# Attention and channel mixing on one core: every engine's order set by a list scheduler inside the kernel, tiles in fixed rings, v loaded once, the gate in place

## The chip, the cores and the metric

The kernel runs on one core of a Trainium2 chip. A core has five engines with instruction queues of their own: TensorE (PE; its weight loads are shown as PEld), VectorE (DVE), ScalarE (ACT), GpSimd (POOL) and SyncE (SP), which here only issues transfers. Each engine works through its queue in order and waits at semaphores for the others. ACT's queue issues transfers too. The metric is the device time of one execution in microseconds, as the median of several runs.

## The reference

Attention over 8 batches of 12 heads with 448 positions of 64 channels, with an RMS norm on q and k; its output, 8 x 448 x 768, goes through a channel-mixing block with a token shift, a squared ReLU and a sigmoid gate.

```python
def _attn_ref(q, k, v, g_q, g_k) -> np.ndarray:
...
    q_n, k_n = (rmsnorm(q, g_q), rmsnorm(k, g_k))
    scale = 1.0 / np.sqrt(q.shape[-1])
    scores = scale * np.matmul(q_n, k_n.transpose(0, 1, 3, 2))
    scores = scores - np.max(scores, axis=-1, keepdims=True)
    attn = np.exp(scores)
    attn = attn / (np.sum(attn, axis=-1, keepdims=True) + 1e-09)
    return np.matmul(attn, v).astype(np.float32)
...
    x_prev = np.concatenate([np.zeros((B, 1, D), dtype=np.float32), x[:, :-1, :]], axis=1)
    xk = mu_k * x + (1.0 - mu_k) * x_prev
    xr = mu_r * x + (1.0 - mu_r) * x_prev
    k = np.maximum(xk @ w_k, 0.0)
    v = k * k @ w_v
    r = 1.0 / (1.0 + np.exp(-(xr @ w_r)))
    return (r * v).astype(np.float32)
```

d_model is 768 and d_ff 1024. mu_r and w_r are drawn with factors 8 and 6.457. The three weight matrices arrive as 64-bit floats; everything else as 32-bit floats.

## The kernel before, in words

To keep precision, every operand of a large matmul is split into a high and a low half of 16 bits, and each product is made of three matmuls: high by high, high by low, low by high. The work falls into three streams.

**Weights.** `weight_tile` (L394) takes one of 20 column tiles in two halves (40 halves): a load of the raw 64-bit words on ACT's queue, three integer operations on DVE that make 32-bit floats of them (L408 to L410, the conversions), a few matmuls and small operations for a scale, and the split into the two halves (L426 to L432).

**Attention.** Two heads are a pair (48 pairs, six to a batch), four heads a quad (24). `prep` (L162) norms q and k of a quad on ACT, POOL and DVE, splits them (`nat`) and turns them with transposing transfers into `stk`. A pair's scores are 7 tiles of 128 x 448, made in four groups of 2, 2, 2 and 1 tiles, with six matmuls each (`group_scores`, L240); the two heads use the two halves of PE's rows. For each tile DVE takes the maximum (L260), ACT the exponent with its sum (L261), DVE the reciprocal (L273, L274), ACT the high half of the scaled probabilities (L279) and DVE the low half (L280), and SP turns both with a transposing transfer into `pT` (L282, L286). `vprep` (L196) scales and splits v; v is held twice, on partitions 0 to 63 and, shifted by one block, on 64 to 127, loaded by three transfers (L157 to L159). `attend` (L299) multiplies `pT` by v in 22 matmuls, 11 for each head side by side, and ACT writes x (L305).

**MoE**, as the code names it. `mix` (L361) makes the shifted mixtures of x, on POOL, DVE and ACT, six for xk and six for xr in a batch (one for each pair), split again. For each of the eight batches, `moe` (L450) makes eight products of xk with w_k (18 matmuls of 448 columns each, L460), which ACT and POOL turn into the two halves of their square through a scratch tile `kf` (L482 to L485), and then, for every block of 128 tokens and half of the columns, a gate product (18 matmuls of 384 columns), three tanh on ACT (L516), a value product (24 matmuls), one DVE operation that joins them (L519) and one on POOL that scales (L520). Two stores on SP write a block. A batch's MoE is 144 matmuls of 448 columns and 294 of 384 on average, 438 in all, 3504 for the eight batches. The first batch has 396 of them and the second 480, since a block that lies across two batches is done with the second.

**The order.** Three generators are stepped by the class `Stream` (L551) on a clock of steps: attention by `ATT_STEPS`, the weights by `W_RATE` and `W_RATE2`, the MoE of a batch `LAG` after its attention. Inside this, the tile framework's own scheduler orders the instructions of each engine; scores get a priority (`QK_PRIORITY`), and `after` (L236) chains the matmuls of one group. `early_mix` makes two of a batch's six xk mixtures after each of its last groups, and the first MoE product may begin with the first two. PSUM has eight banks: four for scores (`sc`), two for the MoE and the weights (`mm`), one for the attention product and small ones (`av`), and one for statistics (`misc`). Scratch tiles are taken from pools that are opened in turn: `pro` until `NA` weight tiles are done, then `mid`, then, after the last weight, `late`. So `kf` has one buffer in batch 0 and two from batch 1 on.

## Time and profile before

| | |
|---|---|
| median of 3 runs | 1216.83 us (1211.75 to 1223.11) |
| the profiled execution | 1216.88 us, of which 1215.1 us from the first to the last instruction (the span) |
| mean granted TensorE clock | 0.934 |
| moved by transfers | 172.77 MB, 142 GB/s on average |
| of these in packets under 512 bytes | 411200 of 456356 packets |

The page of the profile gives totals, forty slices of the span with each engine's busy share in tenths, transfer queues, and groups of instructions with their mean duration and the idle time before them. "Busy" counts an instruction from start to end, so that instructions which overlap on one engine count once. A matmul is shown for longer than the time in which the next can follow it, so PE's pace is read from start to start. For stretches of the span the profile gives busy time by engine, the granted clock (1.00 is full) and the share of the 16 transfer engines.

### The profile page before, as it was taken

Reading aid. Unit: us, or ns where it says so; the run is one execution under the profiler, and the core shown is the slowest. Engines: PE = TensorE matmul, PEld = TensorE weight load, DVE = VectorE, ACT = ScalarE, POOL = GpSimd, SP = SyncE. Lnnn points to the kernel's source line nnn. Section 1 sums busy time; section 2 is a strip of 40 time slices with the busy share of each in tenths; the row PEclk is TensorE's granted clock in tenths of the full one; section 3 lists DMA queues with packets and bytes.
Section 4 is the critical chain, followed back from the end, with each engine's and each line's share of the span. In section 5 each row is a group of like instructions: output and inputs, shape, how many; then the busy total and the mean of one; then the engine's idle time right before and its main releaser. Section 6 shows DMA issues by size and latency. Waiting matters only on the chain. (4 is left out here: it accounts for less than half of the span.)

```text
span 1215.1 us, 18885 instructions
## 1 busy us (share of the span) xinstructions
PE 996.6 (82%) x5935; PEld 476.4 (39%) x5935; DVE 828.9 (68%) x2357; ACT 794.8 (65%) x1756; POOL 672.3 (55%) x678
## 2 busy tenths in 40 slices
PE   1135545686788899999999999999899799999998
PEld 0012222243344344443444444444444354445464
DVE  4577788887977577676877676857775578666200
ACT  3366668677767767677778776777687477865411
POOL 2644357645558645585657564765586257523821
PEclk9996566888989999999999999999999899999999
DMA  7898889978789878878988897797897887885001
GB/s 160 147 182 169 162 165 218 191 152 151 143 139 161 152 123 162 150 129 158 162 154 154 155 170 141 134 167 146 143 157 129 128 148 135 137 158 90 13 14 39
DMA packets 456356, 172.77 MB, mean 142 GB/s; under 512 B 411200, under 2 KB 452672, under 8 KB 456256
## 3 DMA queue, kind: packets, MB, share of 16 engines
q1 hardware_dynamic: 423328, 132.24, 64.2%
q10 hardware_dynamic: 32928, 39.34, 13.8%
q8 instruction: 46, 0.75, 0.3%
q14 instruction: 54, 0.44, 0.1%
HBM read 61.41 MB, written 11.01 MB: 60 GB/s over the span
## 5 line engine op out<-in xcount | busy, mean ns | idle before, releaser
L261 ACT ACTIVATE sc<-sc,sums 128x448 f32<-128x448 f32 x336 | 201.6, 608 | 108.0 <-DVE sums L260 99.4
L280 DVE SCALAR_TENSOR_TENSOR ph<-sc,sums,ph 128x448 f16<-128x448 f32 x336 | 218.3, 677 | 68.4 <-ACT ph L279 66.1
L238 PE MATMUL sc<-stk 64*128 64x448 f16 (+1 forms) x1152 | 190.3, 380 | 68.3 <-DVE ph L280 45.9
L460 PE MATMUL mm<-wvh,kk 128*128 128x384 f16 x896 | 236.5, 332 | 4.0 <-DVE th L519 4.0
L460 PE MATMUL mm<-xk,wkh 128*128 128x448 f16 x768 | 217.8, 363 | 11.6 <-ACT kf L482 10.1
L260 DVE TENSOR_REDUCE sums<-sc 128x1 f32<-128x448 f32 x336 | 196.3, 613 | 37.3 <-PE sc L238 36.7
L279 ACT ACTIVATE ph<-sc,sums 128x448 f16<-128x448 f32 x336 | 195.2, 642 | 31.9 <-DMA pT<-ph 10.1
L238 PE MATMUL av<-pT,vh 128*64 128x448 f16 x672 | 145.8, 387 | 63.4 <-DMA pT<-ph 49.9
L460 PE MATMUL mm<-wrh,xr 128*128 128x384 f16 x672 | 177.1, 327 | 3.1 <-ACT xr L377 2.4
L460 PEld LDWEIGHTS <-kk 128*128 128x128 f16 x1344 | 126.5, 99 | 111.2 <-issue 36.6
L460 PE MATMUL mm<-wvl,kk 128*128 128x384 f16 x448 | 148.9, 332 | 0.0
L460 PE MATMUL mm<-xk,wkl 128*128 128x448 f16 x384 | 139.2, 363 | 0.0
L189 POOL TENSOR_TENSOR nat<-qk,nat 128x896 f16<-128x896 f32 x48 | 91.3, 1903 | 67.6 <-ACT nat L187 67.6
L238 PEld LDWEIGHTS <-stk 64*128 64x128 f16 (+1 forms) x1152 | 56.0, 100 | 184.1 <-issue 138.9
L170 POOL TENSOR_TENSOR xs<-xs 128x448 f32<-128x448 f32 x48 | 55.7, 1160 | 127.1 <-ACT xs L169 126.8
L460 PEld LDWEIGHTS <-xr 128*128 128x128 f16 x1008 | 93.6, 98 | 78.8 <-issue 16.2
L375 DVE SCALAR_TENSOR_TENSOR df<-x,bsc,df 128x448 f32<-128x448 f32 x90 | 90.3, 1014 | 32.7 <-POOL df L374 32.1
L273 DVE TENSOR_SCALAR sums<-sc 128x1 f32<-128x1 f32 x336 | 49.6, 151 | 89.9 <-ACT sc L261 88.5
L182 POOL TENSOR_TENSOR qk<-qk,ss 128x896 f32<-128x896 f32 x48 | 80.1, 1689 | 54.8 <-DVE ss L70 44.7
L460 PE MATMUL mm<-wrl,xr 128*128 128x384 f16 x336 | 109.7, 327 | 0.0
L460 PEld LDWEIGHTS <-wkh 128*128 128x128 f16 x768 | 73.9, 100 | 91.3 <-issue 35.5
L238 PEld LDWEIGHTS <-vh 128*64 128x64 f16 x672 | 59.5, 117 | 113.7 <-issue 67.3
(117 smaller groups left out, 1576.8 us busy)
## 6 DMA issues: line engine op xcount, KB each, us to landing
vf<-in_v_dram SPq DMA_DIRECT2D x48, 224.0 KB, 3.8
qk<-in_k_dram ACTq DMA_DIRECT2D x48, 224.0 KB, 4.8
qk<-in_q_dram ACTq DMA_DIRECT2D x48, 224.0 KB, 5.1
out_dram<-o SPq DMA_DIRECT2D x56, 192.0 KB, 2.9
vf<-in_v_dram SPq DMA_DIRECT2D x48, 192.0 KB, 3.8
raw<-in_moe_w_k_dram ACTq DMA_DIRECT2D x16, 384.0 KB, 4.4
raw<-in_moe_w_v_dram ACTq DMA_DIRECT2D x12, 512.0 KB, 4.4
raw<-in_moe_w_r_dram ACTq DMA_DIRECT2D x12, 384.0 KB, 4.7
```

The source lines that it names most:

```text
L170: nc.gpsimd.tensor_tensor(out=xs[:, :, 0:HD // 2], in0=xs[:, :, 0:HD // 2], in1=xs[:, :, HD // 2:], op=ALU.add)
L182: nc.gpsimd.tensor_tensor(out=tv, in0=tv, in1=spread(y[:, 2 * NT * n:2 * NT * (n + 1)], HD), op=ALU.mult)
L189: nc.gpsimd.tensor_tensor(out=lo, in0=t4, in1=hi, op=ALU.subtract)
L238: return op(**kw)
L260: nc.vector.tensor_reduce(out=sums[:, t:t + 1], in_=sp[:, 0:S], axis=AX.X, op=ALU.max, negate=True)
L261: nc.scalar.activation(out=sp[:, 0:S], in_=sp[:, 0:S], func=AF.Exp, bias=sums[:, t:t + 1], accum_out=sp[:, S:S + 1])
L273: nc.vector.tensor_scalar(out=r[:, j:j + 1], in0=sp[:, S:S + 1], scalar1=1e-9, scalar2=2.0 ** -15, op0=ALU.add, op1=ALU.mult)
L279: nc.scalar.activation(out=ph[:, j, 0:S], in_=sp[:, 0:S], func=AF.Copy, scale=r[:, j:j + 1])
L280: nc.vector.scalar_tensor_tensor(out=ph[:, j, S:], in0=sp[:, 0:S], scalar=r[:, j:j + 1], in1=ph[:, j, 0:S], op0=ALU.mult, op1=ALU.subtract)
L375: nc.vector.scalar_tensor_tensor(out=df, in0=xc, scalar=sc[:, MX + j:MX + j + 1], in1=df, op0=ALU.mult, op1=ALU.add)
L460: nc.tensor.matmul(out=ps_, lhsT=la(i, a), rhs=ra(i, c), start=(i == 0 and a + c == 0), stop=(i == n - 1 and a == 1))
```

## The change

All instructions but those that build an identity matrix now come from generators that yield operations. The class `Plan` holds one clock for each engine. It takes, again and again, the thread whose next operation could start first by those clocks (less a priority), issues it, and moves the engine's clock by a price; `issue_after` pins each instruction behind the last one of its engine, so each engine's queue has exactly this order. A matmul group is issued as one piece: six matmuls for a scores group, 24 for an attention product, six for a piece of an MoE product. Since one line now issues everything, every row of the changed kernel is line 203, and work is told apart by its tiles.

Beside the order:
- Tiles come from rings with a fixed number of buffers (`Ring`). `kf` has one throughout, the output tile `o` two instead of one, the weight scratch two instead of three, q and k four. `pro` and `mid` are gone. Scores have five PSUM banks; attention products, the weights' small products and v's share one (`ot`); the statistics are in SBUF.
- A pair's seventh tile is made together with that of the quad's other pair, 12 matmuls in one group: 7 groups and 8 transposing transfers to a quad, where there were 8 and 10. The number of score matmuls stays.
- v is loaded once, in four transfers of 64 x 4 (or 3) x 64, into 128 x 512 with two blocks of zeros; there are two buffers. ACT's square and cast of it and DVE's split work on 128 x 512 (before: 64 x 896, 128 x 896 and twice 128 x 256). An attention product is 12 pairs of matmuls, not 11.
- q and k are loaded from SP's queue from the third quad on, not from ACT's.
- The gate, the joining operation and the scaling work in the output tile itself; the tile `th` is gone.
- All mixtures are made alike; batch 0 had two POOL operations and one on ACT in place of POOL's and DVE's. A batch's first MoE product is planned when its six xk mixtures are.

```diff
+QK_BUFS = 4
 RAW_BUFS = 2
...
-WF_BUFS = 3
+WF_BUFS = 2
...
+SC_BANKS = 5
+MM_BANKS = 2
+NA = 8
...
+MOE_CHUNK = 2
+VF_BUFS = 2
+VH_BUFS = 2
+KF_BUFS = 1
+XS_BUFS = 1
+NAT_BUFS = 1
...
+    def emit(self, ops):
+        e = ops[0].eng
+        rel = self.ready(ops)
+        s = max(self.clk[e], rel)
+        for op in ops:
+            with self.tc.issue_after(self.last[e].ins) if e in self.last else nullcontext():
+                r = op.fn(op.kw["out"], op.kw["value"]) if op.fn.__name__ == "memset" else op.fn(**op.kw)
+            self.last[e] = r
...
+    def run(self):
+        while self.threads:
+            best, key = None, None
+            for th in list(self.threads):
+                if not isinstance(th[2], list):
+                    if not th[2]():
+                        continue
+                    self.advance(th)
+                    if th not in self.threads or not isinstance(th[2], list):
+                        continue
+                slack = MARGIN if th[2][0].eng == "PE" and th[2][0].form[0] != "moe" else 0
+                k = max(self.clk[th[2][0].eng], th[3] + slack) - (th[1]() if callable(th[1]) else th[1])
+                if best is None or k < key:
+                    best, key = th, k
...
+            self.emit(best[2])
+            self.advance(best)
...
+    def get(self):
+        while not self.free:
+            yield lambda: self.free
+        tag = self.free.pop(0)
+        pool = self.pool() if callable(self.pool) else self.pool
+        t = pool.tile(self.shape, self.dtype, name=tag, bufs=1)
...
+    def put(self, t):
+        tag, name, _ = self.of.pop(id(t))
+        self.plan.use["slot " + tag] = max(x[2] for x in self.plan.use.pop(name))
+        self.free.append(tag)
...
+        "o": Ring(late, [P, D_MODEL], F32, "o", O_BUFS, plan),
+        "wf": Ring(stage, [P, NF, P], F32, "wf", WF_BUFS, plan),
+        "raw": Ring(stage, [P, NF // 2, 2 * P], I32, "raw", RAW_BUFS, plan),
...
+                t = yield from R["qk"].get()
+                for x in range(2):
+                    h0 = 4 * j + 2 * x
+                    yield (A if u < 2 else SP).dma_start(out=t[x * HD:(x + 1) * HD], in_=src[b, h0:h0 + 2].rearrange("h (r t) d -> r h (t d)", t=NT))
+                ts.append(t)
+            LD[u] = ts
...
+    def vload():
+        yield from until(lambda: st.get("vf"))
+        for i in range(NPAIR):
+            b, hp = pairs[i]
+            yield from until(lambda: VFREE)
+            vf = VFREE.pop(0)
+            src = v[b, 2 * hp:2 * hp + 2].rearrange("h (r t) d -> h r t d", t=NT)
+            for h in range(2):
+                for e in range(2):
+                    t = (h + e) % 2
+                    o = NSL * h + (h and not e)
+                    n = (NT + 1 - t) // 2
+                    yield SP.dma_start(out=vf[e * HD:(e + 1) * HD, o:o + n, :], in_=src[h][:, t::2, :])
+            VF[i] = vf
...
+    def scores():
+        for gi, (u, x, t0) in enumerate(groups):
+            yield from until(lambda: 2 * u + x in TQ and len(banks["sc"].free) > 1)
+            both = []
+            for j in range(2):
+                t = yield from banks["sc"].get()
+                both.append(t)
+            ops = []
+            both_pairs = t0 == NT - 1
...
+                for i in (2 * u + 1, 2 * u) if both_pairs else (2 * u + x,):
+                    X = TQ[i]
+                    for h in (1, 0):
+                        hs = slice(h * HD, (h + 1) * HD)
+                        o = i % 2 * HD
+                        n = 1 if both_pairs else 2
+                        ops.append(T.matmul(
+                            form=("t6" if both_pairs else "sc", 3 * S / 2.368),
+                            out=both[h][o:o + HD, 0:S] if both_pairs else both[h][:, 0:S],
+                            lhsT=X[hs, 1, ql * NT + t0:ql * NT + t0 + n].rearrange("p t c -> p (t c)"),
+                            rhs=X[hs, 0, kl * NT:(kl + 1) * NT].rearrange("p t c -> p (t c)"),
+                            start=(m == 0), stop=(m == 2)))
+            yield ops
+            if t0 == NT - 1:
+                R["stk"].put(TQ.pop(2 * u))
+            elif x and t0 == NT - 3:
...
+    def attends():
+        for i in range(NPAIR):
+            yield from until(lambda: CNT.get(i) == 4 and i in VV)
+            x = yield from R["x"].get()
...
+            av = yield from banks["ot"].get()
+            ops = []
+            for j, (pl, hl, c) in enumerate(PASSES):
+                for h in range(2):
+                    ops.append(T.matmul(
+                        form=("av", len(PASSES) * S / 2.368),
+                        out=av[h * HD:(h + 1) * HD, 0:S],
+                        lhsT=(vl if hl else vh)[:, NSL * h + c, :],
+                        rhs=pT[:, NT * pl + (NSL - 1) * h + c, :],
+                        start=(j == 0), stop=(j == len(PASSES) - 1)))
+            yield ops
...
+    def square(f, z, kk, off, KF):
+        kf = yield from R["kf"].get()
+        yield A.activation(out=kf, in_=z[:, 0:S], func=AF.Relu, scale=RSC[:, f:f + 1])
+        banks["mm"].put(z)
+        yield A.activation(out=kk[:, f, 0, off:off + S], in_=kf, func=AF.Square)
+        yield G_.tensor_tensor(out=kf, in0=kf, in1=kf, op=ALU.mult)
+        yield G_.tensor_tensor(out=kk[:, f, 1, off:off + S], in0=kf, in1=kk[:, f, 0, off:off + S], op=ALU.subtract)
+        R["kf"].put(kf)
+        KF[f] = True
...
+    for gen, prio in ((setup(), PRIO_E), (load(), PRIO_E), (mu_stats(), 0), (stats(), PRIO_Q), (preps(), PRIO_Q), (vload(), PRIO_V), (vpreps(), PRIO_V), (scores(), PRIO_S),
+                      (attends(), PRIO_A), (mixk(), 0), (wload(), wprio), (weights(), wprio), (moe(), 0)):
+        plan.spawn(gen, prio)
+    plan.run()
```

Three places show what the order became. On PE, in the middle of the program, where a value product (`mm` from kk and wv) meets the next scores group (`sc` from stk). Before, then now:

```order
L460 LDWEIGHTS kk
L460 MATMUL mm<-wvl,kk 128x384
L238 LDWEIGHTS stk
L238 MATMUL sc<-stk 128x448
L460 LDWEIGHTS kk
L460 MATMUL mm<-wvh,kk 128x384
L460 LDWEIGHTS kk
L460 MATMUL mm<-wvh,kk 128x384
L460 LDWEIGHTS kk
L460 MATMUL mm<-wvl,kk 128x384
L238 LDWEIGHTS stk
L238 MATMUL sc<-stk 128x448
```

```order
L203 LDWEIGHTS stk_6789
L203 MATMUL sc_7234<-stk_6789 128x448
L203 LDWEIGHTS stk_6789
L203 MATMUL sc_7235<-stk_6789 128x448
L203 LDWEIGHTS stk_6789
L203 MATMUL sc_7234<-stk_6789 128x448
L203 LDWEIGHTS stk_6789
L203 MATMUL sc_7235<-stk_6789 128x448
L203 LDWEIGHTS stk_6789
L203 MATMUL sc_7234<-stk_6789 128x448
L203 LDWEIGHTS xr_5057
L203 MATMUL mm_7254<-wrh,xr_5057 128x384
```

Before, one score matmul stands alone, three of the MoE's follow, and then the other five of the group; now the six stand together (the first is just above the piece) and the MoE follows. Counted over the program, PE's matmuls fall into 673 stretches of one kind before and 408 now, of which 518 and 302 lie between the MoE's 438th matmul and the point where 588 are left.

On ACT, at the sixth xk mixture of batch 0 (`xk<-df`), which completes the MoE's first input. `sc<-sc` are exponents, `mm<-raw` conversions of weight halves, `wvh` a weight's high half, `nat` and `xs` q's and k's, `vh` v's, `kf` the first MoE product's result. Before, then now:

```order
L261 ACTIVATE sc<-sc,sums 128x448 x2
L377 CAST xk<-df 128x448
L261 ACTIVATE sc<-sc,sums 128x448
L401 DMA raw<-in_moe_w_v_dram 128x4x256
L187 CAST nat<-qk 128x2x7x64
L279 ACTIVATE ph<-sc,sums 128x448 x2
L407 ACTIVATE mm<-raw 128x512
L401 DMA raw<-in_moe_w_v_dram 128x4x256
L431 ACTIVATE wvh<-wf,WSC 128x8x128
L279 ACTIVATE ph<-sc,sums 128x448
L150 DMA qk<-in_k_dram 64x2x448 x2
L482 ACTIVATE kf<-mm,RSC 128x448
```

```order
L203 CAST nat_1834<-qk_944 128x2x7x64
L203 ACTIVATE x_1790<-ot_1822,bstat 128x448
L203 CAST xk_1403<-df_1714 128x448
L203 ACTIVATE ph_1867<-sc_1796,sums_105 128x448
L203 ACTIVATE ph_1867<-sc_1797,sums_105 128x448
L203 ACTIVATE xs_1895<-qk_1455 128x896
L203 ACTIVATE vh_1862<-vf_94,bstat 128x512
L203 ACTIVATE mm_1924<-raw_1819 128x512
L203 DMA raw_1925<-in_moe_w_v_dram 128x4x256
L203 CAST nat_1922<-qk_1087 128x2x7x64
L203 DMA raw_1950<-in_moe_w_v_dram 128x4x256
L203 ACTIVATE kf_1963<-mm_1934,RSC 128x448
```

Before, 48 exponents and 34 conversions stand ahead of that row, now 56 and 33, and the first `kf` comes ten and nine rows behind it. Loads of q and k (L150) stood in this queue and are gone from here; those of the raw weights stay. On DVE six mixtures, 56 maxima (`sums<-sc`), 52 splits (`ph`), 8 v splits and 32 weight halves stand up to the same point now. Between the sixth and the seventh joining operation of the gate, where PE has its 438th MoE matmul, DVE's two orders have 100 and 108 maxima, 98 and 104 splits, 18 and 24 mixtures, 28 and 16 v splits; all weights are converted by then in both.

On SP, a stretch of the queue, where the transposing transfers (`stk`, `pT`) share it with loads (`vf`, `qk`) and stores. Before, then now:

```order
L157 DMA vf<-in_v_dram 64x2x448
L158 DMA vf<-in_v_dram 64x2x384
L159 DMA vf<-in_v_dram 64x2x64
L191 DMA_TRANSPOSE stk<-nat 128x14x64
L526 DMA out_dram<-o 64x768 x2
L282 DMA_TRANSPOSE pT<-ph 128x14x128
L286 DMA_TRANSPOSE pT<-ph 128x7x64 x2
L282 DMA_TRANSPOSE pT<-ph 128x14x128
```

```order
L203 DMA_TRANSPOSE pT_2129<-ph_2468 128x14x64
L203 DMA_TRANSPOSE pT_2467<-ph_2468 128x14x64
L203 DMA_TRANSPOSE pT_2467<-ph_2469 128x14x128
L203 DMA vf_95<-in_v_dram 64x4x64
L203 DMA_TRANSPOSE pT_2467<-ph_2521 128x14x128
L203 DMA vf_95<-in_v_dram 64x3x64 x2
L203 DMA_TRANSPOSE pT_2467<-ph_2565 128x14x128
L203 DMA vf_95<-in_v_dram 64x4x64
L203 DMA vf_94<-in_v_dram 64x4x64
L203 DMA_TRANSPOSE pT_2619<-ph_2620 128x14x128
```

A v load is now four issues with transposing transfers between them, and loads of q and k stand in this queue as well (88 issues); it has 240 issues for `pT` before and 192 now.

982 lines of the change are left out of this document (543 added, 439 removed).

## The prediction

> **What bounds the kernel now.** I read the busy totals first, then the forty slices, then the span cut into stages, and last the waits. The totals:
>
> ```profile
> PE 996.6 (82%) x5935; PEld 476.4 (39%) x5935; DVE 828.9 (68%) x2357; ACT 794.8 (65%) x1756; POOL 672.3 (55%) x678
> ```
>
> No engine is full over the span, so an average decides nothing. In the slices (each 30.4 us), the reader is to see that PE and DVE take turns:
>
> ```profile
> PE   1135545686788899999999999999899799999998
> DVE  4577788887977577676877676857775578666200
> PEclk9996566888989999999999999999999899999999
> ```
>
> For about thirteen slices PE is half empty and DVE is at 7 or 8 tenths; then PE is at 9 to the end. I cut the span where the MoE's first matmul stands (218 us), where it runs again after a stop for the xr mixtures (310), at its 438th matmul (392; one batch is about 438 of the 3504), and where 588 are left (1098). Columns: length, then busy us of PE, PEld, DVE, ACT and POOL, granted clock, DMA share, GB/s. The second fence has the MoE's matmuls alone.
>
> ```profile
> 0.00:218.00 218.00, 85.05 (x433) 39.31 (x434) 157.26 (x510) 126.85 (x255) 111.23 (x101) 0.78 0.88 174
> 218.00:310.00 92.00, 69.83 (x402) 34.20 (x403) 73.24 (x207) 66.03 (x134) 50.24 (x48) 0.85 0.82 152
> 310.00:392.00 82.00, 71.19 (x431) 33.39 (x428) 63.71 (x167) 57.59 (x132) 51.25 (x52) 0.94 0.86 154
> 392.00:1098.00 706.00, 660.10 (x4014) 308.69 (x4013) 504.54 (x1411) 508.22 (x1154) 413.24 (x425) 0.98 0.84 146
> 1098.00:1215.10 117.10, 110.48 (x663) 60.82 (x661) 30.15 (x67) 36.08 (x85) 46.30 (x54) 0.99 0.20 41
> ```
>
> ```profile
> 218.00:310.00 92.00, 42.11 (x180) 19.02 (x179) 0.85 0.82 152
> 392.00:1098.00 706.00, 464.99 (x2474) 227.77 (x2473) 0.98 0.84 146
> 1098.00:1215.10 117.10, 102.86 (x596) 57.24 (x594) 0.99 0.20 41
> ```
>
> So the first 392 us are paced by the chain through DVE and ACT (attention of batch 0 and all weights, before the MoE can run), and the 706 us behind them by PE, which is busy for 660. What PE costs there is read from these pieces: MoE alone (384 and 448 columns wide), a scores group that cuts into it, a whole attention product and a small one.
>
> ```profile
> 1148.00:1200.00 52.00, 52.00 (x317) 30.75 (x315) 1.00 0.09 23
> ```
> ```profile
> 605.87 0.33 PE L460 MATMUL mm<-wvl,kk 128*128 128x384 f16 x1
> 606.03 0.33 PE L460 MATMUL mm<-wvh,kk 128*128 128x384 f16 x1
> 606.29 0.74 PE L238 MATMUL sc<-stk 64*128 64x448 f16 x6
> 606.97 0.34 PE L460 MATMUL mm<-wvh,kk 128*128 128x384 f16 x1
> ```
> ```profile
> 1125.20 0.35 PE L460 MATMUL mm<-xk,wkl 128*128 128x448 f16 x1
> 1125.39 0.35 PE L460 MATMUL mm<-xk,wkh 128*128 128x448 f16 x1
> ```
> ```profile
> 1125.74 2.21 PE av L238 x21
> ```
> ```profile
> 600.37 0.20 PE L207 MATMUL av<-ident,vs 64*128 64x64 bf16 x1
> ```
>
> From start to start a 384-column matmul is 0.164 us (52/317; most of these are of that width) and a 448-column one 0.19. The six matmuls of a scores group run two at a time, so 0.57 of arithmetic; between the two MoE starts around them lie 0.94 us, where 0.16 would be usual. That leaves 0.2 us for leaving the MoE and coming back: 0.1 for each change of kind. An attention product of 11 pairs is 2.1 us, a small product of v's or the weights' about 0.2.
>
> **Part by part: the first 392 us.** DVE's rows are the prices here (count, then busy us, mean ns, idle before).
>
> ```profile
> L280 DVE SCALAR_TENSOR_TENSOR ph<-sc,sums,ph 128x448 f16<-128x448 f32 x336 | 218.3, 677 | 68.4 <-ACT ph L279 66.1 <-DMA stk<-nat 0.7
> L260 DVE TENSOR_REDUCE sums<-sc 128x1 f32<-128x448 f32 x336 | 196.3, 613 | 37.3 <-PE sc L238 36.7
> L375 DVE SCALAR_TENSOR_TENSOR df<-x,bsc,df 128x448 f32<-128x448 f32 x90 | 90.3, 1014 | 32.7 <-POOL df L374 32.1 <-POOL x L306 0.2
> L218 DVE SCALAR_TENSOR_TENSOR vl<-vf,bstat,vh 128x256 f16<-128x256 f32 x96 | 62.1, 686 | 15.2 <-ACT vh L214 15.1
> L273 DVE TENSOR_SCALAR sums<-sc 128x1 f32<-128x1 f32 x336 | 49.6, 151 | 89.9 <-ACT sc L261 88.5
> ```
>
> Where the MoE begins, at the sixth xk mixture of batch 0, the orders hardly differ: by then DVE has 49 maxima, 46 splits, 14 v splits, 33 weight halves and 1 mixture in the trace, and 56, 52, 8 (of twice the width), 32 and 6 in the new order, since batch 0's mixtures now use DVE. A v split of 512 columns is in no row; it lies between 0.677 (448 columns from PSUM) and 1.014 (448 from SBUF, beside POOL), and I take 0.75. So DVE's 157.3 us become 157.3 + 7 x 0.613 + 6 x 0.677 + 5 x 1.014 - 14 x 0.686 + 8 x 0.75 = 167. At the 438th MoE matmul DVE has 157.3 + 73.2 + 63.7 = 294.2 us behind it; the new order has there 8 maxima, 6 splits and 6 mixtures more (15.1), and 16 wide v splits for 28 (12 - 19.2): 302 us. What changes is not this sum but the share of time that DVE can work at it:
>
> ```profile
> 0.00:60.00 60.00, 8.86 (x41) 4.65 (x42) 29.55 (x113) 19.76 (x28) 29.08 (x26) 1.00 0.82 154
> ```
>
> After these first 60 us, in which loads come in and which I leave as they are, DVE had 264.7 us to do and 332 us passed: 80%. It waited for ACT's exponent (the 88.5 us above, over the span) and for ACT's half of the split (66.1). An order made from the engines' clocks can put other DVE work there, and a fifth scores bank gives it some. I take 90%, with 80 and 95 as ends. The MoE then starts at 60 + (167 - 30)/0.9 = 212 us (218 now), and DVE is through at 60 + 272/0.9 = 362. PE needs from the start to the 438th MoE matmul 438 of them (144 x 0.19 + 294 x 0.164 = 75.6 us), 26 scores groups (14.8), 7 products of 12 pairs (16), 43 small ones (9) and 69 changes (7): 122 us, or 144 at the 0.85 of 218:310, which ends at 356. DVE is last: **362 us** (346 to 400), now 392.
>
> **The 706 us.** New PE work: 2478 MoE matmuls (427 us; 815 of them 448 wide), 134 scores groups (76.4), 34 products (34 x 12 x 0.19 = 77.5), 33 small (6.6), 302 changes (30): 618. The old order by the same prices: 427 + 74.7 + 69 + 6.6 + 518 changes (52) + about 12 for some 100 single score or v matmuls whose partner comes only later = 641, of the measured 706. So 65 us were waits (46 of them as PE idle) or low clock. The twelfth pair of the v product, which now also multiplies a zero half, is in the sum as a loss: 34 x 0.19 = 6.5. Of the 65 I keep half, 33: stretches fall from 518 to 302, and a wait can only stand at the head of one. **651 us** (618 to 683).
>
> **The tail.** The new order ends with 588 MoE matmuls in one stretch: 588 x 0.164 + 144 x 0.026 = 100, plus 6 from the last matmul through DVE, POOL and the store to the end (1208.9 to 1215.1 now). **106 us**, now 117.
>
> **Parts that I cost at nothing.** One kf buffer where two served: the chain that holds it is
>
> ```profile
> L482 ACT ACTIVATE kf<-mm,RSC x64: 616/634/703, 226.3 to 1154.7; 128x448 f32<-128x448 f32 x64
> L483 ACT ACTIVATE kk<-kf x64: 559/577/644, 227.0 to 1155.4; 128x448 f16<-128x448 f32 x64
> L484 POOL TENSOR_TENSOR kf<-kf x64: 924/934/1313, 227.6 to 1156.7; 128x448 f32<-128x448 f32 x64
> L485 POOL TENSOR_TENSOR kk<-kf,kk x64: 1027/1035/2094, 228.7 to 1157.7; 128x448 f16<-128x448 f32 x64
> ```
>
> 3.2 us by medians, against 18 x 0.19 = 3.4 on PE. A POOL step of some 2 us in its way makes it 5, up to 1.8 x 64 = 115 us; attention groups fill PE meanwhile (154 us of them in the 706), so zero to about 15, and zero is taken. If that cover were gone, PE's next MoE product would be late. The gate in place and the statistics in SBUF change no count; more contention with POOL there is bounded by the 1014 against 677 above, and lies inside the 80 to 95%. Half of v's loads fall away and q and k move to SP's queue; SP is a rival below. ACT gets shorter (v squares and casts 512 columns, not 896) and is short of the bound in every stage.
>
> Sum: 362 + 651 + 106 = 1119 us of span. This execution took 1216.88 us for a span of 1215.1, and the median is 1216.83, so 1.8 is added: **1121 us**.
>
> **The clock, weighed.** The row with the lowest clock:
>
> ```profile
> 120.00:180.00 60.00, 30.33 (x153) 14.27 (x152) 49.73 (x170) 38.48 (x81) 25.55 (x23) 0.59 0.82 164
> ```
>
> with PE half idle, against 0.98 where it is full. If batch 0's MoE met this clock, its 122 us would be 207, from 212 to 419, 57 later than DVE: 1178 us. The rows beside it (0.85, 0.94 once the MoE runs) speak for 356, which DVE covers. The Trainium skill, "TensorE: Matmul & The Clock Gate", Part 1, says that after an idle window of about 3.4 us PE runs at half clock until it has been busy for as long; by that rule, at half clock throughout, the same stage would end at 456 and the whole at about 1215, no gain. The trace agrees in direction; no stage in which the MoE runs has a mean below 0.85.
>
> **Rivals.** (1) All waits go: DVE at 95% (346), PE full (618), tail 104: 1070 us. For it: orders are pinned per engine, and nothing is over 85% but PE. Against: semaphores still wait for what really comes late. (2) The shares stay as they were: 400 + 683 + 109, and 1.8: 1194. For it: the old order was fixed per engine too. (3) The low clock, 1178. (4) The other side: SP's queue. It issues in order, and a load that waits for its buffer holds the transposes behind it.
>
> ```profile
> SPq L282 <- DVE ph L280: 113.9, 39, 8.0
> ...
> SPq L157 <- DVE vl L218: 75.6, 29, 9.1
> ```
> ```profile
> L282 SPq DMA_TRANSPOSE pT<-ph x144: 1295/1538/3692, 67.0 to 1117.1; - x144
> ```
> ```profile
> L191 SPq DMA_TRANSPOSE stk<-nat x96: 1228/1594/3721, 41.1 to 1067.9; - x96
> ```
> ```profile
> L150 ACTq DMA_DIRECT2D qk<-in_k_dram x48: 602/620/1769, 1.8 to 979.5; - x48
> ```
>
> New issue time: 144 x 1.54 + 144 x 1.59 + (192 v, 88 q and k, 56 stores) x 0.62 = 659 us. About 120 of these can hold the queue for a buffer (48 v, 44 q and k, 28 stores). The attention would end after 1110, and the kernel at 1217 or later, if each held it for (1110 - 659)/120 = 3.8 us. Today a v load is held 75.6/48 = 1.6 us on average, 2.6 where it is held. So it decides only from more than twice that; two v buffers speak against it, q and k now in the same queue for it.
>
> **Chances.** Forecast (about 1085 to 1160): 0.57. (1) 0.15. (2) 0.12. (3) 0.05. (4) 0.11, of which 0.05 ends within 1% and 0.06 above. About 1% is what a measurement of this kernel can tell from no change. Faster: 0.57 + 0.15 + 0.12 + 0.05 = 0.89. The range goes from 1045 (case 1, less 8 us if the first stage's 24 mixtures take 0.677 and not 1.014, and 15 if a change of kind costs half of what the one place shows) to 1190, inside case 2: about 0.05 lies below; half of case 2 and nearly all of (4), 0.15, above.
>
> **What would show it.** The MoE's first matmul near 212 us and its 438th near 362, with DVE at 90% between; then PE at 95% for some 650 us, 302 stretches with 0.1 us at each change; 588 MoE matmuls alone in the last 106; SP's waits at buffers under 2 us each. It is wrong if the MoE starts in time but then stands (weights, kf or clock), if PE's idle time in the middle is above 46 us, or if transposes land late behind loads.

## The result and the profile after

The changed kernel takes 1183.35 us (median of 4 executions, 1182.68 to 1183.9), the kernel before 1217.65 beside it (4, 1211.75 to 1223.11): a ratio of 0.9719, with a 95% interval from 0.9673 to 0.9765. It is faster by 34 us. 96 were forecast, so the time lies 62 us above the forecast and inside its range, and the gain is about a third of what was expected.

The profiled execution took 1183.67 us for a span of 1181.7. First its totals and three rows of the forty slices (29.5 us each):

```profile
PE 938.7 (79%) x6031; PEld 481.7 (41%) x6031; DVE 870.1 (74%) x2290; ACT 763.0 (65%) x1750; POOL 669.9 (57%) x676
...
PE   1243445486888888989899899898889999899998
...
DVE  5788788899987867886788687886897888773100
...
PEclk9996556597999999999998899999999999999999
```

PE has 58 us less to do than before (996.6), as the grouping of its work promised; but DVE has 41 us more (828.9 before), of which the prediction has 8, in the first stage, and PE's row shows 8 in many slices of the middle where a nearly unbroken row of 9 was forecast. Cut at the places that correspond to those of before (the MoE's first matmul at 231 us, its 438th at 387, 588 left at 1073; columns as before: length, busy us of PE, PEld, DVE, ACT and POOL, granted clock, DMA share, GB/s):

```profile
0.00:60.00 60.00, 12.22 (x53) 6.78 (x53) 41.22 (x128) 20.26 (x33) 27.23 (x28) 1.00 0.69 162
0.00:231.00 231.00, 91.98 (x503) 44.38 (x504) 185.01 (x538) 131.72 (x280) 103.87 (x96) 0.75 0.80 167
231.00:298.00 67.00, 50.32 (x289) 25.20 (x288) 60.38 (x143) 42.11 (x82) 42.16 (x39) 0.83 0.71 144
298.00:387.00 89.00, 75.41 (x496) 37.76 (x495) 73.61 (x190) 62.41 (x151) 50.50 (x53) 0.94 0.81 148
387.00:1073.00 686.00, 618.46 (x4136) 315.71 (x4134) 536.89 (x1398) 502.97 (x1183) 436.04 (x448) 0.98 0.80 143
1073.00:1181.70 108.70, 102.54 (x613) 58.69 (x612) 14.17 (x24) 23.79 (x57) 37.33 (x42) 0.98 0.09 22
```
```profile
60.00:387.00 327.00, 205.49 (x1232) 100.56 (x1233) 277.77 (x744) 215.98 (x478) 169.30 (x159) 0.78 0.81 158
120.00:180.00 60.00, 28.64 (x153) 13.84 (x153) 47.66 (x146) 38.21 (x84) 27.42 (x24) 0.56 0.89 164
```

| stretch | before | forecast | after | missed by |
|---|---|---|---|---|
| start to the 438th MoE matmul | 392 | 362 | 387 | +25 |
| to 588 left | 706 | 651 | 686 | +35 |
| the tail | 117 | 106 | 108.7 | +3 |

At 1073 us the last attention product still lies ahead. The last 588 matmuls themselves start at 1075.4: counted from there the tail takes 106.3 us, as forecast, and the middle 688, 37 too long.

**The middle.** PE works for 618.5 us, where 618 were worked out, but it stands for 67.5 of the 686 us, 22 more than the 46 of before. What it waits for there, before and then after (us in total, times, longest):

```profile
PE av L238 <- DMA pT<-ph: 24.4, 21, 2.7
PE sc L238 <- DVE ph L280: 12.9, 8, 6.8
PE mm L460 <- ACT kf L482: 2.2, 3, 1.3
```
```profile
PE sc L203 <- DVE ph L203: 24.1, 28, 3.9
PE ot L203 <- ACT x L203: 16.8, 13, 2.6
PE mm L203 <- ACT kf L203: 7.8, 8, 2.5
PE sc L203 <- DMA stk<-nat: 5.8, 6, 2.4
PE ot L203 <- DMA pT<-ph: 4.2, 6, 1.5
```

(`ot` is now the bank of the attention product, `av` before, and all instructions have the line of the planner, L203.) The wait for the transposed probabilities is nearly gone, 24 us to 4. In its place PE waits twice as long for a scores bank that DVE's split frees, and for the one `ot` bank, which ACT still reads.

**DVE's 41 us.** Its groups for the statistics of the norm, before and then after (count, busy us, mean ns, idle before):

```profile
L68 DVE TENSOR_TENSOR misc<-misc,ss 128x28 f32<-128x28 f32 x72 | 13.6, 189 | 1.0
L69 DVE SCALAR_TENSOR_TENSOR misc<-misc,ss 128x28 f32<-128x28 f32 x72 | 13.5, 188 | 0.7
L70 DVE SCALAR_TENSOR_TENSOR ss<-misc,ss 128x28 f32<-128x28 f32 x72 | 13.0, 181 | 0.7
...
L176 DVE TENSOR_SCALAR misc<-misc,gm 128x14 f32<-128x14 f32 x24 | 7.0, 293 | 0.3
```
```profile
L203 DVE SCALAR_TENSOR_TENSOR ss<-stm,ss 128x28 f32<-128x28 f32 x72 | 30.7, 426 | 1.2
...
L203 DVE TENSOR_TENSOR stm<-sst,ss 128x28 f32<-128x28 f32 x72 | 27.4, 381 | 1.1
...
L203 DVE SCALAR_TENSOR_TENSOR stm<-stm,ss 128x28 f32<-128x28 f32 x72 | 26.9, 373 | 1.1
...
L203 DVE TENSOR_SCALAR sst<-sst,gm 128x14 f32<-128x14 f32 x24 | 11.8, 491 | 0.0
L203 DVE TENSOR_SCALAR sst<-sst 128x14 f32<-128x14 f32 x24 | 11.2, 466 | 0.0
```

The same instructions, in the same number, take twice as long now that their operands lie in SBUF and not in the bank `misc`. With the two shift operations (9.2 and 7.5 after, 4.5 and 4.4 before) and the row of 172 ns that `sst<-sst` answers to (4.1 before), they take 124.7 us where they took 60.1: 64.6 more. DVE's sum rises by less, since the v splits (62.1 us before) and the mixtures (90.3) take less time in all:

```profile
L203 DVE SCALAR_TENSOR_TENSOR df<-x,bsc,df 128x448 f32<-128x448 f32 x96 | 82.5, 863 | 22.3 <-POOL df L203 21.5 <-POOL x L203 0.5
L203 DVE SCALAR_TENSOR_TENSOR vl<-vf,bstat,vh 128x512 f16<-128x512 f32 x48 | 47.7, 994 | 9.8 <-ACT vh L203 9.2
```

Two pieces of the timeline show where it comes from, DVE's and POOL's of the same microseconds (start, duration):

```profile
923.64 2.00 DVE L203 SCALAR_TENSOR_TENSOR ss<-stm,ss 128x28 f32<-128x28 f32 x1
925.67 0.19 DVE L203 TENSOR_TENSOR stm<-sst,ss 128x28 f32<-128x28 f32 x1
```
```profile
923.51 2.08 POOL L203 TENSOR_TENSOR qk<-qk,gq 128x896 f32<-128x896 f32 x1
925.53 0.10 POOL L203 MEMSET x<- 128x1 f32 x1
```

The DVE instruction that starts just behind a POOL operation of 2.08 us ends with it, 2.00 us later; the next, with POOL free, takes 0.19. Over all 216 multiplications of the Newton steps: the 73 that start while a POOL instruction runs take 0.81 us at the median, up to 2.0. Of these 73, 59 take more than 0.25 us, and each of the 59 ends within 0.15 us of the end of that POOL instruction. The other 143 take 0.18 on average, none above 0.22. With operands in `misc`, before, 71 start beside POOL and average 0.19, none above 0.20. The Trainium skill, "GPSIMD Engine Reference", section 1, lists POOL's SBUF interfaces as shared with VectorE, with contention where a DVE instruction has two SBUF inputs or runs in a 2-port mode. The trace agrees for the multiplications, and gives the size that the page doesn't: here nearly all of them were held for as long as POOL's ran.

### The profile page after: what moved, and what is told of

The parts are those of the page before. It is cut to its first block, busy times and chain, and to the rows that moved or that the text cites. A ratio compares the mean times of both kernels' runs of the same rounds, so it can differ in the third digit from the quotient of the medians.

```text
span 1181.7 us, 18918 instructions
## 1 busy us (share of the span) xinstructions
PE 938.7 (79%) x6031; PEld 481.7 (41%) x6031; DVE 870.1 (74%) x2290; ACT 763.0 (65%) x1750; POOL 669.9 (57%) x676
## 5 line engine op out<-in xcount | busy, mean ns | idle before, releaser
L203 DVE SCALAR_TENSOR_TENSOR ph<-sc,sums,ph 128x448 f16<-128x448 f32 x336 | 216.2, 677 | 62.6 <-ACT ph L203 61.5
L203 ACT ACTIVATE sc<-sc,sums 128x448 f32<-128x448 f32 x336 | 201.5, 619 | 74.5 <-DVE sums L203 73.6
L203 PE MATMUL mm<-wvh,kk 128*128 128x384 f16 x896 | 239.7, 331 | 5.7 <-DVE o L203 3.5
L203 ACT ACTIVATE ph<-sc,sums 128x448 f16<-128x448 f32 x336 | 196.7, 651 | 54.3 <-DMA pT<-ph 40.6
L203 PE MATMUL mm<-xk,wkh 128*128 128x448 f16 x768 | 212.9, 359 | 14.4 <-ACT kf L203 10.8
L203 DVE TENSOR_REDUCE sums<-sc 128x1 f32<-128x448 f32 x336 | 195.3, 615 | 30.3 <-PE sc L203 30.1
L203 PE MATMUL sc<-stk 64*128 64x448 f16 (+1 forms) x1152 | 138.9, 392 | 91.4 <-DVE ph L203 69.7
L203 PE MATMUL mm<-wrh,xr 128*128 128x384 f16 x672 | 179.0, 330 | 1.5 <-ACT o L203 1.2
L203 PEld LDWEIGHTS <-kk 128*128 128x128 f16 x1344 | 127.5, 99 | 113.3 <-issue 36.3
L203 PE MATMUL mm<-wvl,kk 128*128 128x384 f16 x448 | 147.8, 330 | 0.0
L203 PE MATMUL ot<-pT,vh 128*64 128x448 f16 x768 | 130.0, 393 | 21.1 <-DMA pT<-ph 6.7
L203 PE MATMUL mm<-xk,wkl 128*128 128x448 f16 x384 | 137.6, 358 | 0.0
L203 POOL TENSOR_TENSOR nat<-qk,nat 128x896 f16<-128x896 f32 x48 | 92.0, 1916 | 75.8 <-ACT nat L203 75.8
L203 PEld LDWEIGHTS <-xr 128*128 128x128 f16 x1008 | 96.7, 99 | 78.5 <-issue 19.6
L203 PEld LDWEIGHTS <-stk 64*128 64x128 f16 (+1 forms) x1152 | 46.7, 102 | 170.2 <-issue 110.2
L203 PEld LDWEIGHTS <-wkh 128*128 128x128 f16 x768 | 72.5, 99 | 101.5 <-issue 44.5
L203 PE MATMUL mm<-wrl,xr 128*128 128x384 f16 x336 | 110.8, 330 | 0.0
L203 DVE SCALAR_TENSOR_TENSOR df<-x,bsc,df 128x448 f32<-128x448 f32 x96 | 82.5, 863 | 22.3 <-POOL df L203 21.5
L203 DVE SCALAR_TENSOR_TENSOR o<-o,mm 128x384 f32<-128x384 f32 x56 | 30.6, 547 | 87.1 <-PE mm L203 60.0
L203 POOL TENSOR_TENSOR kf<-kf 128x448 f32<-128x448 f32 x64 | 63.1, 985 | 48.5 <-ACT kk L203 48.4
L203 POOL TENSOR_TENSOR qk<-qk,ss 128x896 f32<-128x896 f32 x48 | 82.7, 1723 | 11.8 <-DVE ss L203 8.9
L203 POOL TENSOR_TENSOR o<-o,bsc 128x384 f32<-128x384 f32 x48 | 43.8, 913 | 79.5 <-DVE o L203 51.5
```

The source lines that it names most:

```text
L203: r = op.fn(op.kw["out"], op.kw["value"]) if op.fn.__name__ == "memset" else op.fn(**op.kw)
```

## The experiments

The first theory was: the statistics' bank was traded for a fifth scores bank, and what the fifth bank brings is paid back in held-up statistics. The rival: the list order itself brings less than forecast, and the hold-ups lie beside other waits. In all runs but three the planner or the framework's scheduler makes a new order for the edited kernel, which turned out to matter. Medians; the ratio is to the kernel before in the same session.

### Statistics and banks, with new orders

Four scores banks in place of five, one bank empty, statistics in SBUF:

```diff
-SC_BANKS = 5
+SC_BANKS = 4
-... ("ot", 8 - SC_BANKS - MM_BANKS))}
+... ("ot", 1))}
```

> The changed kernel with four score banks instead of five, one bank left empty, statistics in SBUF. If the fifth bank carries the gain that there was: 1200 us or more, with PE's waits for DVE's low halves at score matmuls above 90 us (now 70). If the bank matters little: 1178 to 1195.

1218.69 us, 1.0021 (0.9997 to 1.0045): 35 above the changed kernel, with PE's waits for DVE's low halves at 93 us, so the first case. Then the same with the statistics in the bank left over, as before the change:

```diff
+    misc = ps.tile([P, 512], F32, name="misc", bufs=1)
-            ss = small.tile([P, NSS], F32, name="sst", bufs=3)
-            tm = small.tile([P, NSS], F32, name="stm", bufs=3)
+            o = (u % 2) * 2 * NSS
+            ss, tm = misc[:, o:o + NSS], misc[:, o + NSS:o + 2 * NSS]
```

> Four score banks, and the statistics in PSUM in a bank of their own, as before the change; all else as changed. Beside it stands the run with four score banks and statistics in SBUF (1219 us). Theory A (statistics in SBUF cost DVE time, and that reaches the end): 1175 to 1195 us, 25 to 45 below 1219, DVE's rows for the statistics near 60 us. Theory B (DVE's lost time is absorbed in this order): 1210 or more.

1185.69, 0.9764 (0.9727 to 0.9802), 33 below the run with the empty bank and the same as the changed kernel within its interval. The instructions are back at their old price:

```profile
L203 DVE SCALAR_TENSOR_TENSOR misc<-misc,ss 128x28 f32<-128x28 f32 x72 | 13.7, 190 | 1.4
...
L203 DVE TENSOR_TENSOR misc<-misc,ss 128x28 f32<-128x28 f32 x72 | 13.6, 189 | 1.3
```

So in these two orders the rest of the change, with the layout of before in PSUM, gains about as much as the whole of it: the trade of the bank nets nothing. A second bank `ot` in place of the fifth scores bank (`SC_BANKS = 4` alone):

> The changed kernel with four score banks and two banks for the attention product, the Gram matrices and the norms, in place of five and one. Against four and one with an empty bank (1218.7 us): if the single attention bank makes PE wait (ot<-ACT x 17 us, ot<-DVE wf 31, dg 21 after), 1195 to 1208; if those waits are covered by other work, 1215 to 1222.

1192.52, 0.9817 (0.9767 to 0.9868), 26 below the empty bank, below the expected 1195 to 1208. But the waits only changed their names: in its middle PE waits 45 us at `ot` for ACT's work on v, and its idle time there is 82 us (705 less 623 busy).

Statistics moved to SBUF in the kernel before, its four banks kept:

```diff
-        ss, tm = misc[:, o:o + NSS], misc[:, o + NSS:o + 2 * NSS]
+        ss = small.tile([P, NSS], F32, name="sst", bufs=2)
+        tm = small.tile([P, NSS], F32, name="stm", bufs=2)
```

> The kernel before the change with this one part of the change alone: the statistics in SBUF. Theory A: the rows for the statistics grow from 60 to about 125 us, the first stage (up to the MoE's 438th matmul, DVE-bound) grows by 20 to 25 us, and the time from 1217 to 1235 to 1260. Theory B: within 8 us of 1217.

1249.33, 1.0284 (1.0249 to 1.0319): 33 us slower, as in theory A, but not where it put them. The first stage grew from 392 to 398 us, the stretch from there to the last 588 matmuls from 708 to 732. With the free bank as its fifth for scores (`bufs=5` at `sc`):

> The kernel before the change with the swap alone: the bank of the statistics given to the scores (five), the statistics in SBUF. With the statistics in SBUF and four banks it took 1249 us. If the fifth bank is worth in the old order what it is in the new one (36 us): 1210 to 1225. If only the new order can use it: 1240 or more.

1298.82, 1.071 (1.066 to 1.0759): another 50 slower; in the order that the old scheduler made of it, the fifth bank brings nothing.

### Keeping the order, statistics beside the attention product

Statistics in the spare columns of the bank `ot`, first with the planner told of PSUM, then with the planner still counting them as SBUF, so that every engine keeps the changed kernel's order but for a few places (4 of PE's 6031 matmuls):

```diff
-            ss = small.tile([P, NSS], F32, name="sst", bufs=3)
-            tm = small.tile([P, NSS], F32, name="stm", bufs=3)
+            o = 512 - 2 * NSS
+            ss, tm = OT[:, o:o + NSS], OT[:, o + NSS:o + 2 * NSS]
```

> The same move of the statistics to PSUM, but the list scheduler knows of it (it no longer makes them wait for POOL in its plan), so the order changes too. Theory A: at least as fast as the one in the old order, 1130 to 1160 us. Theory B: within 8 us of 1183.

> The changed kernel in its own order, but the norm's statistics (sums of squares, their scratch and the Newton steps on them, 28 columns wide) lie in PSUM again, in spare columns of the attention product's bank, as they lay in PSUM before the change. Theory A (DVE's statistics are held up by POOL since they moved to SBUF: 125 us of DVE time for them against 60 before, and this took the gain): these rows fall back to about 60 us, DVE's busy time from 870 to about 805, and the time from 1183 to 1140 to 1160 us. Theory B (DVE is not what is late; the waits come from the single buffer of kf, the single bank for attention products and from the order itself): DVE's busy time falls, but the time stays within 8 us of 1183.

1190.5 (0.9803; 0.9764 to 0.9841) and 1186.81 (0.9781; 0.9741 to 0.982). DVE loses 47 us of busy time, and the kernel gains nothing. New waits stand in the second, on DVE:

```profile
DVE ot L203 <- PE ot L203: 50.1, 21, 7.5
```

The statistics and the matmuls use different columns of this bank, and DVE waits for PE there all the same. Both times lie where theory B puts them, but with these new waits in the way the runs don't separate the two theories.

### The other parts

Without the chain that pins each engine's order (`with nullcontext():` for `issue_after`), so that the framework's scheduler orders the same instructions:

> The changed kernel without the pins: the plan still sets the sequence in which operations are handed over, but the framework's scheduler orders each engine, as before the change. If the plan's order carries the gain: 1205 us or more. If the gain lies in the fewer, larger pieces, rings and banks: within 10 us of 1183.

1274.92, 1.0513 (1.0477 to 1.0548): the pinned order is worth 92 us in this kernel. 79 of them lie in the middle (767 us, PE busy for 680 of them).

Two buffers `kf` (and one `dg`, for the space):

> Two kf buffers instead of one (room made by one buffer less of a weight scratch of 128 columns). In the changed kernel PE waits 13 us for ACT at kf, and ACT 29 us for POOL to give kf back. If the single buffer is one of the waits that replaced the gain: 1165 to 1176 us. If attention groups cover it, as forecast: 1178 to 1188.

1179.01, 0.9709 (0.9684 to 0.9735): 4 us by the medians and 1 by the ratios, within the intervals of the changed kernel, as forecast, and the lowest median of a kernel that does all the work.

### Off DVE, and the planner's prices

The Newton multiplications on POOL:

```diff
-        yield V.tensor_tensor(out=t, in0=a, in1=y, op=ALU.mult)
-        yield V.scalar_tensor_tensor(out=t, in0=t, scalar=-0.5, in1=y, op0=ALU.mult, op1=ALU.mult)
-        yield V.scalar_tensor_tensor(out=y, in0=t, scalar=1.5, in1=y, op0=ALU.add, op1=ALU.mult)
+        yield G.tensor_tensor(out=t, in0=a, in1=y, op=ALU.mult)
+        yield G.tensor_tensor(out=t, in0=t, in1=y, op=ALU.mult)
+        yield G.tensor_scalar(out=t, in0=t, scalar1=-0.5, scalar2=1.5, op0=ALU.mult, op1=ALU.add)
+        yield G.tensor_tensor(out=y, in0=t, in1=y, op=ALU.mult)
```

> The changed kernel with the nine multiplications of each row of statistics issued to POOL (as twelve instructions) in place of DVE; five score banks, one attention bank. Theory (DVE held up on SBUF statistics while POOL is busy costs the ~33 us that the same step cost with four banks): DVE loses about 80 us of busy time, POOL gains 30 to 60, the time falls to 1145 to 1170. Rival (POOL, busy 670 us, makes rows come late instead: chains of twelve dependent POOL instructions behind others): 1180 to 1200, with PE or ACT waiting at stk.

1214.45, 1.0009 (0.9983 to 1.0035), with two `kf` 1209.51, 0.9972 (0.9944 to 1.0):

> The kernel with the multiplications on POOL and two buffers kf (one dg). If both add up: 4 us below the kernel with the multiplications on POOL alone; if not, the same within 2 us.

With two `kf` it is 5 us lower, which fits a sum of the two, but the intervals overlap. The forecast of the first failed and the rival's range was missed too: DVE has 62 us less to do than in the changed kernel (807.7), POOL 76 more (745.5), the first stretch ends 15 us earlier (372), and the middle is 47 longer (735 us to the last 588 matmuls, 688 in the changed kernel). Since POOL's load and the order changed with it, this run doesn't say what lost DVE time costs.

The planner's price, +200 ns for a DVE instruction with SBUF operands alone:

> The changed kernel; in the planner alone, each DVE instruction with all operands in SBUF, more than two columns wide, with two inputs or a scalar operation, is priced 200 ns longer. Theory that the order is off because the planner prices them at 0.18 where they take 0.4 to 0.5 us: 1165 to 1178. Rival (the time of the held-up instructions themselves is what is lost, not the order): 1178 to 1190.

1228.17, 1.0124 (1.008 to 1.0168). No instruction changed, and the other prices gave an order that is 45 us worse. Whether they are nearer to the trace isn't shown: the planner of the changed kernel already lets a DVE instruction without an operand in PSUM start no earlier than 0.19 us before POOL's end (`s = max(s, self.pool_end - 190)`), and the 200 ns come on top. The 45 us cast doubt on the differences of the first group: kernels that the planner orders anew differ by as much for no other reason.

### What PE lacks in the middle

A third buffer `ph` (`X_BUFS` 6, one `dg`), since ACT's wait for its transposes had grown:

> The changed kernel with three buffers ph in place of two (X 6 for 7, dg one, for the space). ACT waited 41 us for ph to be read by its transposes after the change, 10 before. If that holds the score banks and so PE (sc<-DVE ph): 1160 to 1175. If ACT's waits there lie in time that it has to spare: 1178 to 1190.

1228.36, 1.01 (1.0064 to 1.0137): slower by 45, neither case. And three runs with one MoE bank: statistics in the eighth bank, that bank empty, and a sixth scores bank:

```diff
-MM_BANKS = 2
+MM_BANKS = 1
```

> Five score banks, one attention bank, one MoE bank (two before) and the statistics in a bank of their own. If statistics in SBUF cost some 30 us at five score banks too, this stands some 30 us below the same layout with the eighth bank empty; if the fifth score bank leaves room that covers the held-up statistics, less than 10. Against the changed kernel: faster (1150 to 1175) only if the second MoE bank is worth less than the statistics' bank.

> Five score banks, one attention bank, one MoE bank, one bank empty, statistics in SBUF: the control of the run above, and the price of the second MoE bank. If every use of the eighth bank is worth about 30 us (fifth score bank 36, statistics 33, second attention bank 26 so far): 1205 to 1225. If PE seldom has two products of the MoE open: 1183 to 1195.

> Six score banks, one attention bank, one MoE bank, statistics in SBUF. If PE's remaining wait for score banks (24 us in the middle of the changed kernel) is a lack of banks, 15 to 25 us below the run with five and an empty one; if DVE's and ACT's throughput sets it, within 8 of that run.

1365.61 (1.1208; 1.1172 to 1.1245), 1377.36 (1.1309; 1.127 to 1.1348) and 1377.19 (1.1311; 1.1277 to 1.1346). The second MoE bank is worth 194 us against the changed kernel, far outside what was expected. With it gone, the statistics' bank is worth 12 us and a sixth scores bank nothing, but neither price can be carried over: PE then waits at `mm`, in the second run from 390 to 1080 us

```profile
PE mm L203 <- ACT o L203: 40.6, 29, 3.8
PE mm L203 <- DVE o L203: 34.5, 26, 4.3
PE mm L203 <- ACT kf L203: 33.0, 22, 4.3
```

### The statistics priced in the changed kernel's own order

Two kernels plan exactly as the changed kernel and then issue the statistics with one Newton step, or with five, in place of three; all other instructions keep their places.

```diff
-    for _ in range(NEWTON):
+    for n in range(NEWTON):
...
+        for op in (a1, a2, a3):
+            op.skip = skip and n > 0
+            yield op
```
```diff
+        if more and n == NEWTON - 1:
+            a3.more = [(o.fn, o.kw) for o in (a1, a2, a3)] * 2
```

> The changed kernel in the changed kernel's order on every engine, with the second and third Newton step of each row of statistics left out (144 of DVE's 2292 instructions; the inverse square roots are then less exact). At 85.0 us for 216 such instructions they hold DVE some 57 us. If DVE's statistics lie on the path as a whole: 1120 to 1135. If they lie on it about as far as in the runs with four banks (33 us of time for some 60 us of busy time): 1145 to 1160. If other waits take their place: 1172 to 1185. PE's wait for score banks in the middle (sc<-DVE ph 24 us) falls with DVE's load in the first two cases.

> The changed kernel in the changed kernel's order, with two Newton steps more per row of statistics (144 DVE instructions more, some 57 us of busy time), issued right behind the third. On the path as a whole: 1230 to 1245; as with four banks: 1205 to 1220; covered: 1180 to 1192.

1175.53 (0.9677; 0.9634 to 0.972) and 1192.1 (0.9808; 0.9764 to 0.9851). Totals and the first two stretches of the one, then of the other:

```profile
PE 931.2 (80%) x6031; PEld 480.4 (41%) x6031; DVE 824.6 (71%) x2146; ACT 763.4 (65%) x1750; POOL 669.8 (57%) x676
```
```profile
0.00:383.00 383.00, 217.80 (x1285) 107.91 (x1286) 302.54 (x820) 237.83 (x515) 197.34 (x188) 0.81 0.79 161
383.00:1060.00 677.00, 613.50 (x4161) 315.33 (x4160) 507.89 (x1302) 502.79 (x1183) 435.14 (x447) 0.99 0.81 144
```
```profile
PE 934.4 (79%) x6031; PEld 481.4 (41%) x6031; DVE 913.2 (77%) x2434; ACT 763.3 (64%) x1750; POOL 670.6 (57%) x676
```
```profile
0.00:390.00 390.00, 216.91 (x1287) 107.45 (x1288) 330.67 (x925) 236.96 (x513) 197.87 (x188) 0.79 0.78 158
390.00:1080.00 690.00, 617.65 (x4160) 316.71 (x4158) 568.36 (x1486) 503.57 (x1186) 435.36 (x448) 0.99 0.79 142
```

88.6 us of DVE's busy time lie between the two, and 16.6 us of time (about 8 to 24 by the two intervals): 0.19 us per us of DVE. The third of the expected cases holds: other waits take the place. The wait for a scores bank in the middle goes from 24.5 to 30.5 us between them, no more. If the same rate holds for the 64.6 us of held-up statistics, they cost the changed kernel an estimated 12 us (6 to 17), and not the 33 that the re-planned pairs show.

## Why the prediction was right, and where it was wrong

**PE's work: right.** The count of matmuls, groups and changes of kind gave 618 us for the middle, and PE was busy for 618.5. The half microsecond is luck, since the sum and the busy time are not quite the same measure: by the same prices the old middle was 641, and PE was busy for 660. But the price of a change is borne out by the trace after: 22 steps from a MoE matmul of 384 columns to a score matmul without a wait take 0.259 us at the median, against 0.163 between two such MoE matmuls. The tail of 588 matmuls was right (106 against 106.3).

**The waits in the middle: wrong, and the largest miss (35 us).** The step that failed is "Of the 65 I keep half, 33", with its reason that a wait can only stand at the head of one of fewer stretches. By the prediction's own prices 706 - 641 = 65 us were not work before, and 686 - 618 = 68 are not work now: none of the 65 went. PE's idle time alone is 67.5, which the prediction had named as a sign of its failure (above 46). The waits that fell were those that the old order made (24 us for transposes); what came are waits at buffers that come round again, a scores bank, the single attention bank and `stk`, and PE meets these in fewer stretches as well. In no kernel run here that is ordered by the planner is PE's idle time in the middle below 63 us (677 - 613.5, with one Newton step). DVE's load is a small part of what holds it up there: 60.5 us of it more, with five Newton steps against one, make 13 us of stage. Whether a better order of the same instructions would remove it is open: a third `ph`, a second attention bank in place of the fifth scores bank, and other prices each led the planner to an order that was worse, and no run gave the fixed order another bank.

**The first stage: wrong by 25 us.** The steps that failed are "I take 90%" and "DVE is last". The MoE starts at 231 us, not 212, and the 438th matmul stands at 387; so 19 of the 25 us are lost before the MoE starts, and from there on the clock was much as before (0.83 and 0.94 in the rows from 231 and from 298 us, 0.85 and 0.94 before). DVE's sum was too small as well: 319 us up to the mark (41.2 + 277.8) where 302 were worked out. Its statistics take 45.6 of these, and the same 117 instructions before 22.3. A wide v split, taken at 0.75 us, took 0.994. By its busy time DVE was at 277.8 of 327 us, 85%, near what was said; but the share follows the work and doesn't set the time: with one, three and five Newton steps DVE is busy for 81, 85 and 87% from 60 us on, and the stage ends at 383, 387 and 390. So 28 us of DVE work between the first and the last make 7 us of time in the profiled executions. What PE waits for until 388 us, before and then after:

```profile
PE sc L238 <- DVE ph L280: 33.0, 19, 6.0
PE av L238 <- DMA pT<-ph: 25.5, 8, 8.0
PE sc L238 <- DMA stk<-nat: 18.0, 1, 18.0
PE av L416 <- DVE wf L410: 15.4, 4, 8.1
PE av L421 <- DVE dg L420: 8.1, 11, 1.8
```

```profile
PE sc L203 <- DVE ph L203: 45.7, 17, 5.1
PE ot L203 <- DVE wf L203: 31.3, 9, 12.3
PE ot L203 <- DVE dg L203: 21.5, 14, 4.1
PE ot L203 <- ACT x L203: 16.2, 8, 4.0
```

A busy sum divided by a share would set the time if DVE were always fed; here it is one link of chains over PE, ACT and transposes. Three of the four rows after are at the bank `ot`, through which the weights' Gram matrices and attention products pass one at a time. That its single bank is the cause was not shown: with two (and four scores banks, in another order) the mark came at 383 us, 4 earlier.

**"The gate in place and the statistics in SBUF change no count": true, and yet not free.** The count is the same and their time doubles. The bound taken for it, 1014 against 677 (a factor of 1.5), came from a wide operation; a narrow one of 0.19 us can become 2.0. It cost DVE 64.6 us, and the kernel an estimated 12. The line of the changed planner that waits for POOL's end was a sign of it that the prediction passed over.

**The fifth scores bank.** It was a reason for the 90%. The bank is worth 35 us against an empty one in re-planned kernels, but so are the two other uses of it (33 for the statistics, 26 for `ot`), and the one that the change gave up is about what it got. All three lie within the 45 us by which a new order alone moved the time, so none of them is a sure price.

**Costed at nothing, rightly:** one buffer `kf`, 4 us at most; the loads of v and of q and k on SP's queue, since none of PE's rows above names such a load, and the waits for `stk` behind the queue cost it 6 us in the middle. SP's waits were longer than the 2 us named (69 for DVE's `sums` take 152.5 us, 2.2 each), but PE's wait for `pT` in the middle fell from 24.4 to 4.2, so the queue, case (4), didn't decide. The clock stood at 0.56 from 120 to 180 us, but at 0.98 in the middle, where the MoE runs in bulk, so that rival didn't decide. Of the rivals, (2), the shares stay as they were (1194), came nearest: it is 11 us off, the forecast 62. In the middle its 683 us are near (686) and so is its mechanism, that as much is lost to waits as before; in the first stage its 400 us are 13 too many.

So the 62 us are 25 in the first stage and 37 between it and the last 588 matmuls. An estimated 12 of them are the held-up statistics. The rest of the middle is waits that were forecast to go and came back under other names; why they stay at this level, and what sets the end of the first stage in DVE's place, isn't settled.

## What to carry to other kernels

A sum of busy time over a share is a forecast only where adding work to that engine lengthens the stage by about as much; test it with more and less work in the same order, before believing in the engine. Moving small operands from PSUM to SBUF beside a busy POOL doubled the time of such DVE instructions here, so price it per instruction and not per count. Where a planner sets the order, compare edits with the order held fixed: a new order alone moved this kernel by 45 us.

## What the runs showed of the hardware

A DVE instruction of 28 columns with all its operands in SBUF and two inputs that starts while POOL runs takes 0.81 us at the median, and in one case 2.00, ending with the POOL operation; with an operand in PSUM it takes 0.19 either way. Reductions from SBUF are not held: of the 48 `sst<-xs` after, the 38 that start beside POOL take 0.61 us at the median and 0.62 at most, as do the other ten. POOL's twelve instructions for the same three steps took 214 to 245 ns each at the median, up to 1.2 us (least, median and greatest stand ahead of the times of the first and last start):

```profile
L203 POOL TENSOR_TENSOR stm<-sst,ss x72: 239/244/676, 28.3 to 1003.6; 128x28 f32<-128x28 f32 x72
...
L203 POOL TENSOR_SCALAR stm<-stm x72: 210/214/766, 29.8 to 1004.3; 128x28 f32<-128x28 f32 x72
```
